# One more transpose by DMA: chunk 1's second row in a fused gated linear attention and bilinear feed-forward kernel

## The chip, the cores and the metric

The kernel runs on one core of one Trainium2 chip. The time is device microseconds (us) of one execution; three executions of the kernel before took 191.68, 191.82 and 191.87 us, median 191.82. The core has engines that each run their own instructions in order: TensorE (PE in the profile, its weight loads PEld), VectorE (DVE), ScalarE (ACT), GpSimd (POOL) and SyncE (SP, which here only issues transfers). Engines wait for one another through semaphores. Transfers are carried by 16 DMA engines, which the queues of SP, POOL and ACT share.

## The reference

The first part is a recurrence over 768 tokens for each of 4 batch rows and 8 heads, with a 48x48 state for each head; the second is a bilinear feed-forward over all 3072 tokens.

```python
def _attn_ref(q, k, v, alpha):              # each (4, 8, 768, 48), float32
    state = np.zeros((B, H, D, D), dtype=np.float32)
    for t in range(S):
        state = alpha[:, :, t, :, None] * state + np.einsum('bhd,bhe->bhde', k[:, :, t], v[:, :, t])
        y[:, :, t] = np.einsum('bhd,bhde->bhe', q[:, :, t], state)
    return y

def _moe_ref(x, w_a, w_b, w_out):           # x: (3072, 384); w_a, w_b: (384, 1536); w_out: (1536, 384)
    a = x @ w_a
    b = x @ w_b
    return a * b @ w_out
```

## The kernel before, in words

The recurrence is done in chunks. A chunk is 256 tokens (128 partitions of two tokens each) of two batch rows, called row 0 and row 1 of the chunk (`u` in the code); there are six chunks, numbered 0 to 5. Even chunks hold batch rows 0 and 1, odd ones rows 2 and 3, and chunks 2 and 3 follow 0 and 1 in time. For each chunk the kernel takes logarithms of alpha, sums them along the tokens on TensorE, raises them to decay factors, multiplies queries and keys with these, turns queries and keys so that the head dimension lies on partitions, forms masked scores, and adds the part inside the chunk and the part carried by the state. The result is evicted as the bf16 tile `xT`, and the feed-forward of that chunk follows: 12 blocks of 128 hidden columns, each with an `a` product, a `b` product, an elementwise product of both, and at last four output products with `w_out`.

The order of the work is written out. `PROGRAM` is a text in which every line names a chunk and lists its steps; the loop at L1033 emits them one by one, and each engine executes its own in that order. A step's letters V, S, P, Y say which engine runs it (VectorE, ScalarE, GpSimd, SyncE); a number at the end names the PSUM bank where a TensorE step writes. A step that writes a bank waits until the readers of what was there are done. The steps that matter here, with the functions that emit them:

- `ld a 0 P`, `ld k * Y`: load alpha, k, q or v of row 0, row 1 or both (`*`); L515. Row 0a and 0b in chunk 0 are halves of the heads. Loads of `W` (w_a, w_b; L495) and `Wo` (w_out; L498) are issued by POOL.
- `ln` (L522, ACT): logarithms. `l2`, `l2s` (L530, L579): sums over token pairs. `H`, `L`, `R`: their split into high and low parts. `B`, `A2`, `AQ`: running sums on TensorE. `E .. b` and `E .. i` (L633, ACT): decay factors and inverse factors. `ra` (L611, ACT) and `lv` (L618): the level of a token's first half. `dk`, `de`: decay of a whole sub-chunk.
- `mk`, `mq` (L644, DVE): multiply keys and queries into `QKp`.
- `C u h` (L704) turns half the heads of one row with eight TensorE transposes into a PSUM bank; `Ce u h` (L928 on DVE, L926 on ACT) evicts that bank into `kqT`. `T u` (L713) turns a whole row instead by one DMA transpose issued by SP from `QKp` into `kqT`, and `Tr u` reorders its keys into the tile `kp` (L928 or L926). In the kernel before, chunks 0 and 1 use `C` and `Ce`, chunks 2 to 5 use `T` and `Tr`.
- `v`, `vs` (L737 or L739, L926 or L928): values as bf16 and their swapped copy. `K`, `K2` (L760, L773): state products, `k` (L787, L790, L791): state update on DVE.
- `D u h` (L805): scores. `M` (L814): masked eviction on DVE; or `Mc` (L818, ACT) and `Mm` (L822, DVE) in two steps. `SB`, `SA`, `Y` (L834): the parts of the attention output. `X` (L870 on ACT, L872 on DVE): eviction to `xT`.
- `a f w`, `b f w` (L889): feed-forward products of block f, of one row of tokens (`a 3 0`: 128x256, a half product) or both (`a 3 *`: 128x512). `as` (L895, ACT) evicts `a`; `pr` (L903, DVE) multiplies it with `b` out of PSUM. `o m h` (L911): output product of token block m, first or second six blocks. `ot` (L926, L928) evicts it, `st` (L944, SP) stores it. `oc`, `otc`, `stc` do the same for the last block in two column halves.
- `fill`: products of zeros in the first microseconds.

Which of the two queues a load stands in decides what it follows. POOL executes its arithmetic steps (`lv`, `l2`) and its load issues in one order, so a load behind an `lv` on POOL is issued only when that `lv` has its operands. SP's queue holds transposes, stores and the later loads, and an issue behind a `T` waits until that `T` was issued.

## Time and profile before

| | before |
|---|---|
| median of three executions | 191.82 us (191.68 to 191.87) |
| the profiled execution | 191.33 us, of which its span is 189.5 us |
| TensorE busy | 183.1 us (97% of the span) |
| VectorE busy | 135.3 us (71%) |
| ScalarE busy | 117.2 us (62%) |
| GpSimd busy | 57.7 us (30%) |
| moved by DMA | 29.41 MB |

The profile shows one execution. Busy time of TensorE includes the modelled end of each product in a pipeline, so a busy TensorE is not one at its peak; how fast it really goes is read from when one group of products starts after the other in the timeline. The profiled execution took 0.49 us less than the median of the three others.

### The profile page before, as it was taken

The page shows a single profiled execution, that of the slowest core. Times are in us where ns is not written, and L with a number is a line of the kernel's source. Part 1 is how long each engine was busy: PE and PEld are TensorE (multiplying, and loading weights), DVE is VectorE, ACT ScalarE, POOL GpSimd, SP SyncE. Part 2 cuts the span into 40 slices and gives each one's busy share as a digit, 9 for nine tenths or more (in the row PEclk, how much of TensorE's full clock was granted, in tenths as well). Part 3 has the DMA queues.
Part 4 walks back from the last instruction along what each step waited for, and adds up shares of the span by engine and source line. Part 5 has one row for each costly group of instructions (what it writes and reads, how often), then busy time and mean ns, then how long its engine had stood idle before and what let it go on. Part 6 is the DMA issues. An engine that isn't in the chain of part 4 may idle for free.

```text
span 189.5 us, 6112 instructions
## 1 busy us (share of the span) xinstructions
PE 183.1 (97%) x2597; PEld 114.6 (60%) x2613; DVE 135.3 (71%) x246; ACT 117.2 (62%) x220; POOL 57.7 (30%) x81
## 2 busy tenths in 40 slices
PE   7999899999999999999999999999999999999993
PEld 3888676656688776644457544646446454545563
DVE  2477778679898999797899898995287753144511
ACT  4497586896978996667475979747625524320610
POOL 8999177985154000203930226002000000000000
PEclk9999999999999999999999999999999999999999
DMA  5999999999999799988999396926902100002123
GB/s 130 265 223 199 263 241 248 237 258 268 236 220 194 102 190 263 266 231 154 208 267 206 93 159 134 127 85 71 175 27 83 45 3 0 0 5 83 42 83 125
DMA packets 64475, 29.41 MB, mean 155 GB/s; under 512 B 55760, under 2 KB 62816, under 8 KB 64448
## 3 DMA queue, kind: packets, MB, share of 16 engines
q1 hardware_dynamic: 46080, 16.34, 40.9%
q0 software_dynamic: 18224, 12.58, 38.8%
q8 instruction: 20, 0.33, 0.7%
q10 hardware_dynamic: 144, 0.10, 0.2%
q14 instruction: 7, 0.06, 0.1%
HBM read 25.98 MB, written 4.74 MB: 162 GB/s over the span
## 4 chain that ended last, share of the span: by engine, by line
PE 88%; DMA 4%; DVE 3%; issue 2%; POOL 2%; ACT 1%; POOLq 0%; ACTq 0%
PE psum L889 47%; PE psum L911 24%; PE psum L834 6%; DMA a_t<-in_alpha_dram 4%; PE psum L805 2%; PE psum L704 2%; PE psum L599 1%; DVE prod L903 1%; PE psum L922 1%; PE psum L773 1%; PE psum L760 1%; PE psum L666 1%; PE psum L557 1%; PE psum L558 1%; DVE vx L928 1%
## 5 line engine op out<-in xcount | busy, mean ns | idle before, releaser
L889 PE MATMUL psum<-xT,wb_t 128*128 128x512 bf16 (+1 forms) x261 | 54.7, 335 | 1.1 <-DVE vx L928 0.4
L889 PE MATMUL psum<-xT,wa_t 128*128 128x512 bf16 (+1 forms) x264 | 54.7, 336 | 0.4 <-issue 0.2
L911 PE MATMUL psum<-wo_t,prod 128*128 128x384 bf16 x276 | 49.2, 326 | 0.1
L889 PEld LDWEIGHTS <-wa_t 128*128 128x128 bf16 x270 | 25.8, 98 | 20.1 <-issue 0.2
L889 PEld LDWEIGHTS <-wb_t 128*128 128x128 bf16 x270 | 25.6, 98 | 19.6 <-DMA wb_t<-in_moe_w_b_dram 0.7
L911 PEld LDWEIGHTS <-prod 128*128 128x128 bf16 x276 | 26.2, 98 | 17.9
L926 ACT ACTIVATE ot<-psum 128x384 f32<-128x384 f32 (+1 forms) x12 | 5.7, 478 | 17.9 <-PE psum L911 15.3
L618 POOL TENSOR_TENSOR q_t<-q_t,ra 128x384 f32<-128x384 f32 x7 | 7.0, 1007 | 28.0 <-ACT ra L611 26.9
L926 ACT ACTIVATE vx<-v_t 32x384 bf16<-32x384 bf16 x28 | 14.6, 521 | 0.5
L579 POOL TENSOR_TENSOR l<-la 64x384 f32<-64x384 f32 x6 | 6.0, 994 | 26.0 <-PE psum L889 11.3
L818 ACT ACTIVATE m<-psum 128x768 bf16<-128x768 f32 x14 | 11.0, 810 | 3.2 <-PE psum L805 3.1
L928 DVE COPY ot<-psum 128x384 f32<-128x384 f32 (+1 forms) x13 | 7.0, 536 | 7.5 <-PE psum L911 7.0
L814 DVE TENSOR_TENSOR m<-psum,mask 128x768 bf16<-128x768 f32 x10 | 9.5, 952 | 1.8 <-PE psum L805 1.2
L522 ACT ACTIVATE la<-a_t 128x1536 f32<-128x1536 f32 (+2 forms) x9 | 9.4, 1053 | 2.0 <-DMA a_t<-in_alpha_dram 2.0
L870 ACT ACTIVATE xT<-psum 128x768 bf16<-128x768 f32 x10 | 7.9, 811 | 4.1 <-PE psum L834 3.9
L644 DVE TENSOR_TENSOR QKp<-q_t,beta 128x768 bf16<-128x768 f32 x10 | 9.4, 952 | 0.6 <-POOL q_t L618 0.6
L644 DVE TENSOR_TENSOR QKp<-k_t,invb 128x768 bf16<-128x768 f32 x10 | 9.6, 968 | 0.4 <-ACT invb L633 0.2
L834 PE MATMUL psum<-m,vx 64*64 64x64 bf16 (+1 forms) x576 | 8.7, 205 | 0.0
L515 POOL DMA_DIRECT2D v_t<-in_v_dram x8 | 8.7, 1087 | 0.0
L834 PEld LDWEIGHTS <-vx 64*64 64x64 bf16 x576 | 7.6, 108 | 0.6 <-issue 0.5
L737 ACT ACTIVATE vx<-v_t 128x768 bf16<-128x768 bf16 x9 | 7.5, 838 | 0.3 <-DMA v_t<-in_v_dram 0.2
L822 DVE TENSOR_TENSOR m<-m,mask 128x768 bf16<-128x768 bf16 x14 | 7.4, 551 | 0.4 <-ACT m L818 0.3
(278 smaller groups left out, 300.5 us busy)
## 6 DMA issues: line engine op xcount, KB each, us to landing
out_dram<-ot SPq DMA_DIRECT2D x23, 192.0 KB, 2.0
q_t<-in_q_dram SPq DMA_DIRECT2D x3, 768.0 KB, 6.0
k_t<-in_k_dram SPq DMA_DIRECT2D x3, 768.0 KB, 12.1
a_t<-in_alpha_dram POOLq DMA_DIRECT2D x2, 768.0 KB, 11.9
v_t<-in_v_dram POOLq DMA_DIRECT2D x4, 384.0 KB, 8.2
a_t<-in_alpha_dram SPq DMA_DIRECT2D x2, 768.0 KB, 6.7
a_t<-in_alpha_dram POOLq DMA_DIRECT2D x3, 384.0 KB, 7.8
k_t<-in_k_dram POOLq DMA_DIRECT2D x3, 384.0 KB, 7.4
```

The costliest lines, as they stand in the source:

```text
L515: eng.dma_start(out=t[:, us, hs].rearrange("p b h r d -> p (b h) (r d)"), in_=src[ch.b0 + us.start:ch.b0 + us.stop, hs, ch.s * 2 * C:(ch.s ...
L522: nc.scalar.activation(out=ch.la[:, us, hs].rearrange("p b h r d -> p (b h r d)"), in_=ch.a[:, us, hs].rearrange("p b h r d -> p (b h r d) ...
L644: eng.tensor_mul(QKp[ch.c % 2][:, u, j, :, hs, :D], src[:, u, hs].rearrange("p h r d -> p r h d"), f)
L737: nc.scalar.activation(out=o_, in_=i_, func=AF.Copy)
L814: nc.vector.tensor_mul(m, x, maskn())
L818: nc.scalar.activation(out=m, in_=x, func=AF.Copy)
L834: nc.tensor.matmul(o, lhsT=lhsT, rhs=rhs, start=(g, c) not in begun, stop=False, skip_group_check=True)
L870: nc.scalar.activation(out=o_, in_=i_, func=AF.Copy)
L889: nc.tensor.matmul(p, lhsT=(wa_t, wb_t)[w][:, kk, f * 128:(f + 1) * 128], rhs=ch.xT[:, kk, us, :], start=(kk == 0), stop=(kk == KT - 1))
L911: nc.tensor.matmul(op, lhsT=ch.prod[:, f, at:at + C], rhs=wo_t[:, f, :], start=(f == 0), stop=(f == NFF - 1))
L926: nc.scalar.activation(out=o_, in_=i_, func=AF.Copy)
L928: eng.tensor_copy(o_, i_)
```

## The change

The functions are the same; only `PROGRAM` differs. For chunk 1's row 1 the steps `C 1 1`, `C 1 0`, `Ce 1 1 V` and `Ce 1 0 V` are gone, and `T 1` (a DMA transpose on SP) and `Tr 1 V` (on DVE) take their place. Chunk 2's keys (`ld k *`) are no longer loaded from POOL's queue but from SP's, behind that transpose. The loads of chunk 3's alpha and values, and of its queries and keys, stand later in the order. Besides, every step has been placed anew: order, PSUM banks and, for some 60 steps, the engine. Counted over the whole text, VectorE takes over from GpSimd a net six `lv` and four `l2` or `l2s`, ScalarE takes over from VectorE `vs` and `ot` steps, and the `X` steps are distributed anew. The feed-forward products, their shapes and their number are the same.

The diff, cut to the first 25 us or so of the kernel, to chunk 1's attention, and to the loads that move:

```diff
-0: ld q 0b Y; B 0a 0; E 0b i; mk 0b V; ld v 0 P; ld q 0a Y; ld a 1 P; cs 0 m P; ld k 1 P; ld q 1 P; cm 1; E 0b b; dk 0 2; E 0a i; mq 0b V; C 0 1 3; W b 0 256; cz 0 v P
-0: ld v 1 P; mk 0a V; E 0a b; fill 2 0; W a 256 768; cz 1 q P; W a 0 256; mq 0a V; C 0 0 1; Ce 0 1 S; Ce 0 0 V; K 0 0 0; de 0; W b 256 768; D 0 1 2; D 0 0 4; cs 1 m P; ln 1
-0: k 0 0 V; SB 0 0
-1: ld a 0 P
-0: v 0 S; vs 0 1 S; B 1a 6; E 1a i; M 0 0
-1: ld a 1 P
-0: E 1a b; W a 768 1536; c2 P; vs 0 0 V; B 1b 4; W b 768 1536; dk 1 6; E 1b i; M 0 1
-1: ld q 0 P
-0: Y 0
-1: ld k 0 P
-0: mk 1a V; SA 0; E 1b b; mq 1a V; mk 1b V; C 1 0 7; K 1 1 2; mq 1b V; Ce 1 0 V; C 1 1 3; v 1 S; Ce 1 1 V; de 1; K 1 0 4; k 1 0 V; k 1 1 V; D 1 0 6; X 0 S
-0: a 2 0 0; a 4 0 1; Mc 1 0; vs 1 1 V; as 4 0; vs 1 0 V; a 5 0 3; D 1 1 4; Mc 1 1; SB 1 6; Mm 1 1 V; a 1 0 1; Mm 1 0 V; b 4 0 2; as 1 0; pr 4 0; a 3 0 4; as 3 0
-0: b 0 0 1; K 0 1 5; SA 1; Y 1; a 0 0 2; as 2 0; b 2 0 0; k 0 1 V; X 1 S; b 3 0 4; pr 3 0
-1: ln 0; l2 0 P
...
+0: B 0a 0; ld q 0b Y; E 0b i; E 0b b; mk 0b V; ld v 0 P; ld q 0a Y; ld a 1 P; cs 0 m P; mq 0b V; ld k 1 P; ld q 1 P; fill 2 2; cm 1; W b 0 256; E 0a i; dk 0 3; mk 0a V
+0: E 0a b; cz 0 v P; C 0 1 2; Ce 0 1 S; mq 0a V; C 0 0 0; Ce 0 0 V; ld v 1 P; de 0; W a 256 768; cz 1 q P; K 0 0 1; ln 1; D 0 1 4; D 0 0 2; k 0 0 V; SB 0 0; M 0 0
+0: v 0 S; vs 0 1 S; dk 1 6; de 1; M 0 1; W a 0 256; B 1a 2; vs 0 0 S; E 1a b; mq 1a V; W b 256 768; E 1a i; mk 1a V; B 1b 4; E 1b i; mk 1b V; Y 0; E 1b b
+0: SA 0; X 0 V; C 1 0 2; v 1 S; vs 1 1 S; K 1 0 3; K 1 1 4; cs 1 m P; a 5 0 5; as 5 0; Ce 1 0 V; D 1 0 0; Mc 1 0
+1: ld a 0 P
+0: a 3 0 2; as 3 0; mq 1b V; C 1 1 5; vs 1 0 S; k 1 0 V
+1: ld a 1 P
+0: a 0 0 3; W a 768 1536; a 4 0 0; as 4 0; k 1 1 V; a 1 0 2; Ce 1 1 V; SB 1 4; Mm 1 0 V; D 1 1 6; Mc 1 1; Mm 1 1 V
+1: ln 0
+0: b 3 0 0; pr 3 0; b 5 0 1; pr 5 0; a 2 0 6; c2 P; as 0 0; SA 1; W b 768 1536
+1: ld q 0 P; l2 0 P
+0: Y 1; X 1 V; b 2 0 7; b 1 0 0
+1: ld k 0 P
+0: b 0 0 1; pr 0 0
...
-2: ld k * P
...
-3: ld v * P
...
-3: ld a * P
-1: mk 1 V; D 0 1 4; M 0 1
...
-1: C 1 1 2; C 1 0 4
-0: ot 3 V
-1: Ce 1 1 V
...
-1: K2 1 1 5 7; Ce 1 0 V; D 1 1 2; Y 0; v 1 S; SA 0
...
+1: Y 0; mk 1 V; mq 1 V; T 1; SA 0; K2 1 1 2 3; X 0 S; v 1 V; vs 1 0 S; vs 1 1 S
+0: o 3 1 -
+1: a 7 0 4; a 9 0 5; a 10 0 6; as 10 0; k 1 0 V; k 1 1 V
+2: l2s 0 V
+0: c3 P
+1: a 2 0 2; b 9 0 3
+2: ld k * Y; ld v * P
+0: o 2 0 7
+1: b 2 0 6
+0: ot 3 S; st 3 Y
+1: b 10 0 0
+2: l2s 1 V; l2 0 V; R 0
+1: as 2 0; pr 2 0; as 7 0; pr 10 0
+0: ot 1 S
+2: ra 0; lv 0 q P
+1: b 7 0 2
+2: ra 1
+1: pr 7 0; a 6 0 4; as 6 0; b 6 0 6; pr 6 0; as 9 0
+3: ld a * P
+0: o 2 1 -; ot 2 S
+1: a 0 0 2; Tr 1 V
+3: ld v * P
+1: as 0 0
+0: cs 1 0 P
+1: pr 9 0; b 0 0 0
+2: R 1
+1: D 1 1 4; SB 1 6; pr 0 0
+0: st 0 Y
+1: Mc 1 1; Mm 1 1 V; a 1 0 1; as 1 0; a 4 0 2; as 4 0; a 3 0 3; as 3 0; D 1 0 4; M 1 0
+2: AQ 0; E 0 b; E 0 i; lv 1 k V
+1: b 1 0 2; b 4 0 3; pr 4 0
...
```

## The prediction

> **What bounds the kernel now.** I read the page's busy shares first, then the chain that ended last, then who waited, and last the timeline of the first 25 us.

> ```profile
> PE 183.1 (97%) x2597; PEld 114.6 (60%) x2613; DVE 135.3 (71%) x246; ACT 117.2 (62%) x220; POOL 57.7 (30%) x81
> PE 88%; DMA 4%; DVE 3%; issue 2%; POOL 2%; ACT 1%; POOLq 0%; ACTq 0%
> ...
> PE psum L540 <- DVE og L440: 1.2, 1, 1.2
> PE psum L889 <- issue: 0.5, 3, 0.2
> PE psum L889 <- DVE vx L928: 0.4, 1, 0.4
> ```

> TensorE is the bound: it is 88% of the chain, and all its waits come to 2.3 us. From about 22 us to its end at 186.5 us, group follows group in the timeline: a half product starts 0.33 us after the last, a full one 0.65, an output group of six 0.98. So a change can gain only by taking products from TensorE or by getting through the first 22 us sooner, and it loses wherever TensorE begins to wait. The other engines have little in hand:

> ```profile
> core 0: us, PE busy (x) PEld busy (x) DVE busy (x) ACT busy (x) POOL busy (x), PEclk, DMA share, GB/s
> ...
> 40.00:50.00 10.00, 10.00 (x186) 6.62 (x185) 9.50 (x17) 8.09 (x13) 5.70 (x7) 1.00 1.23 257
> 50.00:60.00 10.00, 10.00 (x160) 8.01 (x159) 9.05 (x19) 8.83 (x21) 3.66 (x4) 1.00 1.39 219
> 60.00:70.00 10.00, 10.00 (x158) 8.08 (x156) 9.41 (x25) 9.15 (x20) 1.43 (x2) 1.00 0.97 140
> ```

> VectorE is 91 to 95% busy here, and from 40 to 60 us the DMA share is above 1: more transfers are outstanding than 16 engines carry. The granted clock is 1.00 throughout, so no step below turns on it.

> **The change, part by part.** *1. The sixteen transposes.* Chunk 1's `C 1 1` and `C 1 0` leave TensorE:

> ```profile
> 45.09 1.06 PE L704 MATMUL psum<-ident,QKp 128*128 128x128 bf16 x16
> 45.98 1.14 PE L911 MATMUL psum<-wo_t,prod 128*128 128x384 bf16 x6
> 45.86 1.28 DVE L928 COPY kqT<-psum 128x1024 bf16<-128x1024 bf16 x2
> ```

> In the chain they are 0.89 us, by the neighbours' starts 0.85 to 1.0. They lie on the path: −0.9. DVE loses 1.3 us of evictions and gains `Tr 1` (kp row, 0.51), and is not the bound.

> *2. The first 25 us.* I lay the new order end to end, each step from its operands on and at the spacing at which the same step follows another here.

> ```profile
> 9.16 1.02 ACT L926 ACTIVATE kqT<-psum 128x1024 bf16<-128x1024 bf16 x1 [0.52 <-PE psum L704]
> 12.34 0.61 DVE L928 COPY vx<-v_t 32x384 bf16<-32x384 bf16 x2
> 13.41 0.87 ACT L633 ACTIVATE prod<-psum 128x384 f32<-128x384 f32 x2
> 16.76 0.81 ACT L870 ACTIVATE xT<-psum 128x768 bf16<-128x768 f32 x1
> 18.09 1.16 PE L889 MATMUL psum<-xT,wa_t 128*128 128x256 bf16 x9
> 20.57 0.50 PE L889 MATMUL psum<-xT,wb_t 128*128 128x256 bf16 x3 [0.43 <-DVE vx L928]
> ```

> The rows are the first `Ce`, `vs 0 0`, the first factors of row 1, `X 0`, the first feed-forward products, and the first `b`, which waited for w_b. In the new order both fills (0.27 each) and `dk 0` stand ahead of `C 0 1`, so `Ce 0 1` starts at 9.7, not 9.16. ACT then does `de 0`, `ln 1` (10.95), `v 0`, `vs 0 1`, `de 1`, and at 13.9 `vs 0 0`, which DVE did before and which costs ACT 1.05. So row 1's first factors start at 15.0, not 13.4. DVE multiplies at 15.4, 15.9 and 16.4 and does `X 0` from 16.9 to 17.8; `a 5 0` starts at 17.85, near the 18.09 of before. But `D 1 0` and `C 1 1`, which stood ahead of it, now come after it. `D 1 0` waits 0.3 for `Ce 1 0`; `Y 1` waits 0.45 for `D 1 1`, `Mc 1 1` (0.81) and `Mm 1 1` (0.47). At 24.8 us the new order has finished 12 half products with `K 0 1` to come, the old one 12.4 with `K 0 1` done. That is 0.13 + 0.37 = 0.5, and a bank that `pr 5 1` frees 0.1 late: +0.55. Ends: −0.1 if the 0.7 us that TensorE lost before about the first `b` is won in full, +1.2 with whole durations in place of spacings.

> *3. More joints.* TensorE changes from long products to groups of 64x64 products 30 times in place of 27; one such group costs 0.06 to 0.25 more than its products (`SB` alone 0.14). Part of this is in step 2: +0.2 (0 to 0.6).

> *4. The new wait.* `T 1` starts when `mq 1` ends. Laid out on from step 2, TensorE reaches `Y 0` at 46.05 us and DVE does `M 0 1`, `mk 1` and `mq 1` (0.88 each) from 44.75 to 47.4. On SP's queue nothing is ahead of it; behind it stand chunk 2's keys, two stores, the decay rows of chunk 2 and its own transposes. On DVE, `pr 9 0`, `R 1` and `pr 0 0` stand behind `Tr 1`, and TensorE's `D 1 1` needs `Tr 1`. TensorE has `Y 0`, `SA 0` and `K2` (1.2 together), three output groups and twelve half products before it: 1.2 + 2.9 + 3.9 = 8.0, so it arrives at about 54.1, and `T 1` has to land by 53.6. The rows of a transpose and of a crowded DMA:

> ```profile
> 129.10:136.90 7.80, 7.64 (x83) 4.00 (x71) 2.94 (x4) 5.62 (x10) 0.99 (x2) 1.00 0.95 137
> 48.00:52.00 4.00, 4.00 (x74) 2.49 (x63) 3.52 (x7) 3.90 (x8) 0.25 (x1) 1.00 1.50 233
> DMA to landing us min/median/max: 4.4/4.7/4.8
> ```

> The landing row is the transposes' own; two of them, nearly alone, held the 16 engines 0.95 of 7.8 us, some 3.6 us each. At 47.4 chunk 2's queries (issued at 37.2, landing 11.1 us later) and then its values are still in flight; the values take some 2.7 us. Sharing engines, both are through at 48.3 + 2.7 + 3.6 = 54.6. `Tr 1` then ends at 55.1, and `D 1 1` is 1.0 late: +1.0. Ends: 0 if it lands in 4.8 us; +2 if the values and a store go first as well. This cover is the only one that the change adds and the only one that I think fails. [...]

> *5. Everything else.* Chunk 2's keys follow `T 1` on SP; loads behind a transpose landed 3 us apart there, so at about 57.7, and `lv 1 k` on DVE is due at about 58: 0, with the failure as a rival. The later loads of chunk 3 are hidden by some 5 us of other work each; if that cover went, ACT's `ln` would be late and with it `AQ`. Moved steps add to DVE six `lv` (0.555), four `l2`/`l2s` (0.57), two `v` (0.35), one `X` (0.96), one `Tr` and take four `vs` (0.53), five `ot` (0.55) and two `Ce` (0.69): +1.5 us in all. ACT gets some 6 us more and POOL 13 less, both below their share; the end (last eviction and store, 186.5 to 189.5) is as before. Costed at 0 (0 to +1).

> Sum: −0.9 + 0.55 + 0.2 + 1.0 = +0.85 us. The profiled execution's 191.33 becomes 192.18; the median stands 0.49 above it, so 192.67, forecast **192.7 us**.

> **Rivals.** *The transpose is hidden* (faster or equal). `T 1` lands in the 4.4 to 4.8 us of its row; it decides at 6.2 us after issue. For it: one of the eight transposes went out at 57.9 us, beside a load, and its queue was free again 3.07 us later. Against it: the share of 1.50. Without step 4 the sum is −0.15; with step 2 at its low end −0.8; the middle, −0.45, gives 191.4. [...]

> *The keys are late too* (slower still). If `T 1` lands at 54.6 and chunk 3's alpha, which POOL issues once `ra 0` is done, shares the engines from 55.5 on, the keys land at about 60, not 57.7. DVE stops at `lv 1 k`, `pr 1 0` behind it does not free its bank, and TensorE stops at `a 11 0`: +1 to +2, 193.7 to 194.7. Against it: half of the alpha's issue may come late enough.

> *VectorE becomes the bound.* 91% from 40 to 130 us and +1.5 us with less idle to place it in: a few short waits that are not won back, +1 to +2 without step 4's wait; 193. Against it: the evictions that leave are in that very stretch.

> That the change does not do what it says is excluded: sixteen transposes are gone from TensorE's list and one DMA transpose more is on SP's.

> **How the numbers follow.** Forecast (+0.4 to +1.4): 0.36. Hidden: 0.42, of which 0.28 faster by over 0.2% (0.38 us, about what a measurement of this kernel can tell from no change) and 0.14 within. Keys late: 0.16. VectorE: 0.06. The low ends of the forecast and of VectorE's case lie within 0.2% with 0.04 more. So faster 0.28, same 0.18, slower 0.54. Range 191.2 to 194.4: below it a tenth (the hidden case with step 2 at its low end), above it a tenth (late keys at their upper end). The forecast's own range is 192.2 to 193.2.

> **What would show it.** Step 1: 48 rows of L704 transposes in place of 64, and nine transposes on SP. Step 2: `X 0` on DVE near 17 us, and a gap in TensorE's starts before `Y 1`. Step 4: `kp` on DVE waiting for the transpose by name, a landing above 6 us, and TensorE's scores of chunk 1's row 1 behind it. The prediction is wrong if TensorE's starts have no gap between 45 and 60 us, or if it is behind by more than 1 us at 25 us.

## The result, and the profile after

The changed kernel took 197.4 us at the median of four executions (196.25 to 200.21), the kernel before 191.84 beside it: a ratio of 1.0257 (95% interval 1.0209 to 1.0305). The ratio leaves out the execution of 200.21 us, which is over 1.5% above the fastest. By it the change is slower by 4.9 us, where 0.85 was forecast, and outside the range of 191.2 to 194.4 us. In its first profiled execution the granted TensorE clock stood at one half for 6.8 us, and that execution is the 200.21; so the same kernel was profiled once more, and what follows is from that second profile unless it says otherwise.

> The changed kernel once more, with nothing edited. Its first profile had the granted clock at one half from about 13 to 20 us, while its other runs (196.3 to 198.0 us) had a clock of 1.0; so a profile at full clock is wanted. Theory W (three waits that the new order makes): 196.5 to 197.5 us again, and at full clock TensorE loses about 1.3 us more than before up to the first feed-forward product, 1.5 at `a 9 *` near 33 us, 1.5 at `1 o 3 1` near 78 us, 0.6 at `3 Y 1` and 1.2 at chunk 4's `D 1 0` near 130 us. Rival C (the clock): the half-clock stretch comes back in the profile, and it is the loss: 2.8 us or more of the 5 lie at `B 1a` and `B 1b`.

Measured: 196.5 us (195.7 to 198.4), ratio 1.0227 (1.0164 to 1.0290); the profiled execution is the 198.4. First its page: the span, the busy shares, the clock by fortieths of the span, the chain that ended last, and the group of the output products.

```profile
span 196.6 us, 6102 instructions
...
PE 186.8 (95%) x2597; PEld 115.1 (59%) x2597; DVE 135.1 (69%) x245; ACT 123.8 (63%) x234; POOL 44.7 (23%) x66
...
PEclk9988999999999999999999999999999999999999
...
PE 86%; DMA 3%; ACT 3%; issue 2%; DVE 2%; SPq 1%; DVEq 0%; ACTq 0%
...
L904 PE MATMUL psum<-wo_t,prod 128*128 128x384 bf16 x276 | 50.0, 326 | 2.0 <-issue 2.0
```

The half clock is not the whole of the loss: two of these executions had a mean clock of 1.0 and took 195.7 and 196.2 us. So rival C above, that the clock is the loss, falls as the only cause.

VectorE, ScalarE and GpSimd are all less than 70% busy: none of them has become the bound. In the chain TensorE's share fell from 88% to 86%, and "issue", time in which TensorE waited for nothing that the profile shows, ends 2.0 us ahead of output products. The busy time by stretch of the same run:

```profile
core 0: us, PE busy (x) PEld busy (x) DVE busy (x) ACT busy (x) POOL busy (x), PEclk, DMA share, GB/s
10.00:14.00 4.00, 3.54 (x95) 3.05 (x93) 2.87 (x4) 3.90 (x9) 4.00 (x8) 0.88 1.31 219
14.00:18.00 4.00, 4.00 (x66) 3.77 (x66) 1.14 (x3) 2.62 (x7) 3.95 (x6) 0.69 1.38 200
...
40.00:50.00 10.00, 9.46 (x222) 5.94 (x220) 9.12 (x20) 7.02 (x12) 1.15 (x1) 1.00 1.29 220
50.00:60.00 10.00, 10.00 (x135) 7.33 (x135) 8.58 (x18) 8.63 (x22) 3.96 (x4) 1.00 1.16 216
60.00:70.00 10.00, 10.00 (x152) 8.22 (x145) 9.04 (x20) 9.08 (x20) 1.96 (x3) 1.00 1.11 144
74.00:82.00 8.00, 6.57 (x162) 4.39 (x164) 6.84 (x14) 5.48 (x10) 0.00 (x0) 1.00 1.25 274
```

From 50 to 60 us, where the forecast put its 1.0 us of waiting, TensorE is busy throughout. It idles from 74 to 82 us instead, where the kernel before was busy 7.95 of the 8.00 us. The chain there, in the changed kernel:

```profile
78.12 0.69 PE psum L827 x60
78.81 0.76 PE psum L904 x4
79.57 1.43 issue
80.99 0.50 PE psum L904 x2
```

TensorE stops in the middle of one output group: four of its six products are issued, then nothing for 1.43 us, then the last two. The profile finds no semaphore that these two waited for.

To find all such places, each group of products was measured from its start to the next group's start, less the usual spacing of its kind (0.328 us a half product, 0.648 a full one, 0.975 an output group, and so on); what is left over is lost time. By stage, from the two profiles:

| stage (us, roughly) | lost before | lost after | what it is |
|---|---|---|---|
| to 17 | 4.15 | 6.24 | `B 1a`, `B 1b` at half clock, 0.98 + 0.90; the rest in the first steps |
| 17 to 39 | 1.22 | 1.90 | many small waits |
| 39 to 76 | 0.74 | 1.61 | 0.61 at 44.0, 0.58 at 49.3: issue |
| 76 to 83 | 0.33 | 2.03 | 1.75 at 79.2: issue |
| 83 to 125 | 0.88 | 1.55 | 0.92 at 107.5: issue |
| 125 to 146 | 0.23 | 2.07 | 1.16 at chunk 4's `D 1 0`; the rest in small waits |
| later | 0.40 | 0.18 | |
| sum | 7.95 | 15.58 | +7.6 |

The products themselves are 1.0 us less. So the end of TensorE's work comes 6.6 us later in this execution, some 1.7 of it by the clock (`B 1a` and `B 1b` took 2.28 and 2.20 us, in before 1.25 and 1.55), 3.9 by issue, 1.2 by chunk 4's `D 1 0`.

### The profile page after: what moved, and what is told of

It is laid out like the page before. It is cut to its first block, busy times and chain, and to the rows that moved or that the text cites. A ratio compares the mean times of both kernels' runs of the same rounds, so it can differ in the third digit from the quotient of the medians.

```text
span 198.4 us, 6102 instructions
## 1 busy us (share of the span) xinstructions
PE 188.1 (95%) x2597; PEld 116.4 (59%) x2597; DVE 136.2 (69%) x245; ACT 123.8 (62%) x234; POOL 44.0 (22%) x66
## 4 chain that ended last, share of the span: by engine, by line
PE 79%; DMA 7%; DVE 5%; ACT 2%; issue 2%; POOL 1%; SPq 1%; POOLq 0%; DVEq 0%; ACTq 0%
PE psum L882 42%; PE psum L904 23%; PE psum L827 5%; DMA a_t<-in_alpha_dram 4%; DMA bl<-row 3%; PE psum L798 2%; DVE prod L896 2%; PE psum L550 1%; PE psum L551 1%; PE psum L659 1%; PE psum L915 1%; PE psum L766 1%; PE psum L592 1%; DVE l L523 1%; SPq L937 1%
## 5 line engine op out<-in xcount | busy, mean ns | idle before, releaser
L882 PE MATMUL psum<-xT,wa_t 128*128 128x512 bf16 (+1 forms) x270 | 55.8, 337 | 1.3 <-DVE prod L896 1.3
L882 PE MATMUL psum<-xT,wb_t 128*128 128x512 bf16 (+1 forms) x270 | 56.3, 337 | 0.6 <-ACT as__467 L888 0.3
L919 ACT ACTIVATE vx<-v_t 32x384 bf16<-32x384 bf16 x40 | 20.8, 520 | 0.7
L919 ACT ACTIVATE ot<-psum 128x384 f32<-128x384 f32 (+1 forms) x17 | 8.2, 483 | 11.7 <-PE psum L904 8.5
L611 POOL TENSOR_TENSOR q_t<-q_t,ra 128x384 f32<-128x384 f32 x3 | 3.0, 1014 | 36.3 <-ACT ra L604 36.3
L863 ACT ACTIVATE xT<-psum 128x768 bf16<-128x768 f32 x9 | 7.1, 813 | 6.2 <-PE psum L827 6.1
L921 DVE COPY ot<-psum 128x384 f32<-128x384 f32 (+1 forms) x8 | 4.2, 528 | 8.6 <-PE psum L904 8.6
L827 PE MATMUL psum<-m,vx 64*64 64x128 bf16 (+1 forms) x576 | 8.9, 208 | 0.5 <-issue 0.5
L572 POOL TENSOR_TENSOR l<-la 64x384 f32<-64x384 f32 x3 | 3.0, 995 | 28.2 <-ACT la L515 28.2
L827 PE MATMUL psum<-kqT,Sm 64*64 64x128 bf16 x144 | 7.8, 219 | 0.0
## 6 DMA issues: line engine op xcount, KB each, us to landing
out_dram<-ot SPq DMA_DIRECT2D x23, 192.0 KB, 4.0
```

Of the source, the lines that this page charges most:

```text
L827: nc.tensor.matmul(o, lhsT=lhsT, rhs=rhs, start=(g, c) not in begun, stop=False, skip_group_check=True)
L863: nc.scalar.activation(out=o_, in_=i_, func=AF.Copy)
L882: nc.tensor.matmul(p, lhsT=(wa_t, wb_t)[w][:, kk, f * 128:(f + 1) * 128], rhs=ch.xT[:, kk, us, :], start=(kk == 0), stop=(kk == KT - 1))
L919: nc.scalar.activation(out=o_, in_=i_, func=AF.Copy)
L921: eng.tensor_copy(o_, i_)
```

## The experiments

**Which part of the new order loses.** Three kernels join the two orders: each takes its first steps from one and the others, in their own sequence, from the other.

```diff
# e2: first 177 steps of before (32 us), then the rest in the order of after
# e3: first 127 steps of after (25 us), then the rest in the order of before
# e4: first 204 steps of after (38 us), then the rest in the order of before
```

> The order of before for its first 177 steps (to about 32 us of the span), the new order for everything behind them. Theory W: the lead-in's 1.3 us and the 1.5 at `a 9 *` are gone, the waits near 78, 109 and 130 us stay: 197.4 - 2.8 = 194.6 us. Rival E (everything is lost early, the later waits only show slack that an early loss made): about 192 us. Rival L (all of it is lost late): 197 us.

> The new order for its first 127 steps (to about 25 us of the span), the order of before for everything behind them; the DMA transpose is not in it. Theory W: 191.8 + 1.3 = 193.1 us. Rival C: 195 us or more, with the clock at one half between 13 and 20 us in some runs. Rival L: 191.8 us.

> The new order for its first 204 steps (to about 38 us of the span), the order of before for everything behind them; the DMA transpose is not in it. Theory W: 191.8 + 1.3 + 1.5 at `a 9 *` = 194.6 us. Rival E: 197 us. Rival L: 191.8 us.

Measured: e2 198.1 us, ratio 1.0239 (1.0172 to 1.0307); e3 193.8, ratio 1.0071 (1.0037 to 1.0105); e4 195.9, ratio 1.0171 (1.0112 to 1.0230). The new first 25 us alone cost 1.4 us by the ratio: 0.7 to 0.9 in the five executions whose mean clock was 1.0 (their mean is 192.9 us, against a mean of 192.2 and a median of 192.0 for before), and about 2.2 in the five where it was 0.991 (194.0 to 194.5). So theory W has the order's own part about right, and theory C has a part too. Rival L, by which e3 and e4 would have stayed at 191.8 us, falls with both. e2 keeps all of the loss though its first 32 us are those of before: theory E falls. Not all of e2 tells of the change, though. At its seam TensorE lost 1.9 us (`b 8 *`, `a 6 *`); its wait near 78 us was 2.20 us, and behind it the clock stood at one half for 3.4 us. e4 loses 1.2 us at a seam of its own kind and had the half clock in three of four executions; its sum can't be divided further.

**Code loading.** In the wait at 79 us (1.43 us) the profile shows nothing that was missing, which leaves the instruction itself. The page's DMA part has a queue of that name:

```profile
q8 instruction: 20, 0.33, 0.7%
```

Twenty packets of 16,384 bytes, which the trace places all along TensorE's run; its 2597 products and 2597 weight loads are 20.3 times 256. TensorE's instructions were numbered in order (matmuls, weight loads, and the few that only wait or drain), and the four issue waits of the changed kernel fall at numbers 1216, 1472, 2496 and 3264; in its first profile at 2496 (1.5 us) and 3264 (0.65); in e2 at 2496 (2.20). All of these numbers are 192 more than a multiple of 256. A packet's transfer ends 1.73, 1.29, 1.32 and 1.55 us before TensorE goes on. The theory F that follows: code comes in blocks of 256 instructions; where a block's instructions run out sooner than the next block's transfer ends, TensorE stands still. When a block is asked for no trace had shown; that it is when the one before is entered, as the forecast for e5 has it, was the author's assumption. In the changed kernel's first profile small products (64x64, in `D`, `K2`, `SB`, `Y`: some 9 to 17 ns for each matmul with its weight load) made the block ahead of number 2496 pass in 4.1 us (77.4 to 81.5); a block of feed-forward products alone took 25.7 (158.2 to 183.9). The sharpest test shifts the blocks and leaves all work where it is:

```diff
 def ff(ch, w, f, us, i):
-    for kk in range(KT):
-        nc.tensor.matmul(p, lhsT=..., rhs=ch.xT[:, kk, us, :], ...)
+    for part_ in two halves of the columns if ch.c == 0 and n == 4 * C:   # e5: in before, 12 groups
+        for kk in range(KT):                                             # e8: in after, f in (6, 7, 8), 6 groups
+            nc.tensor.matmul(p[:, part], lhsT=..., rhs=ch.xT[:, kk, part_, :], ...)
```

> The order of before, not one step moved; the twelve full products of chunk 0 (three matmuls of 512 columns each) are issued as six matmuls of 256 columns each. The same work, 72 more instructions on TensorE before 44 us. Theory F (code loading): TensorE's instructions come in blocks of 256, the next block is asked for when one is entered, and with the DMA engines full it is usable about 5.8 us later; a block whose 256 instructions run through sooner leaves TensorE without instructions ('issue' in the waits). Shifting the block boundaries of before by 72 puts blocks 10 and 13 onto its small products: by its own start times 3.3 + 3.5 us of waits near 81 and 106 us, 0.3 near 50: 191.9 + 7 = 199 us (195 to 201, as part of it can be won back by loads that come earlier). Rivals W and C (the wait belongs to the new order, its transfers or its clock, not to the code): 191.9 to 192.3 us, since nothing that they speak of changes.

> The changed kernel, not one step moved; six of chunk 0's full products are issued as six matmuls of 256 columns instead of three of 512: 36 more instructions on TensorE before 36 us, the same work. Theory F, by the changed kernel's own start times: the waits for code near 44, 49 and 79 us shrink from 0.3, 1.1 and 1.5 us to 0, 0 and 1.0, one of 1.1 us is new near 136 us: 196.4 - 0.8 = 195.6 us, with the wait at `1 o 3 1` moved to another operation, 36 instructions earlier. Rivals W and C: 196.4 us and the wait at `1 o 3 1` as before.

Measured: e5 194.5 us, ratio 1.0127 (1.0077 to 1.0176); e8 195.6, ratio 1.0169 (1.0130 to 1.0207). The kernel before, with no step moved, became 2.4 us slower by the ratio through 72 instructions. The split in itself does not explain that: by the spacings above, two half products take 0.656 us and a full one 0.648, so twelve split groups cost an estimated 0.1 us. Its chain near 105 us:

```profile
104.30 1.46 PE psum L834 x67
105.76 1.58 issue
107.34 0.30 PE psum L834 x5
```

Its issue waits of 0.91, 0.56, 0.40 and 1.80 us are at numbers 704, 1728, 2752 and 3520, again 192 more than a multiple of 256; before has none above 0.45. The size was missed (7 us forecast, 2.4 measured, outside 195 to 201), because the forecast counted a block's time from when TensorE enters it. The transfers show that the next block is asked for earlier: in the changed kernel, in stretches of long products, its packet runs up to 3.9 us before TensorE enters the block at whose entry it was supposed to be asked for. In e8 the waits at 44, 79 and 107 us are gone, and 0.70 us at number 1472 is left. The same stretch as above, in e8:

```profile
77.89 0.69 PE psum L827 x60
78.59 1.08 PE psum L909 x6
79.67 0.63 PE psum L592 x12
```

The output group's six products are issued without a break. In the profiles e8 ends 1.8 us sooner (span 194.8 against 196.6, the same half clock at 13 us in both). Not all that the code waits cost came back: they shrank by 3.2 us (3.9 to 0.7), and the end by 1.8. Part of the rest stands in the same profile: TensorE, now sooner at chunk 3's small products, waits 0.87 us at 101.5 us for a transpose and VectorE's copy of it, a wait that the changed kernel does not have. Rivals W and C said nothing would change in either kernel; they fall for this part.

**Why a block comes late.** Two readings were left: the DMA engines are full (share 1.25 there), or the block is run through too fast.

```diff
-4: ld a * Y          (SyncE's queue, issued at 70 us)
 0: st 1 Y
+4: ld a * Y          (issued at 74.2 us)
```

> The changed kernel with one load issued later: chunk 4's alpha (768 KB, some 2.9 us of all 16 DMA engines) goes out on SyncE's queue behind the store near 83 us, not at 70 us. Theory F1 (the code block comes late because the DMA engines are full): the ninth code block is fetched 3 to 4.5 us after it is due instead of 5.6, TensorE's wait at `1 o 3 1` shrinks from 1.75 to 0.6 us or less, 196.2 - 1.1 = 195.1 us. Theory F2 (the block is run through too fast, whatever else is transferred): the wait stays at 1.2 us or more, and the time at 196.2 us.

Measured: 195.9 us, ratio 1.0186 (1.0135 to 1.0237). The load went out at 74.2 us, sooner than the text before the run has it, but behind chunk 3's queries and a store. The profiled execution is the slowest of the six (199.2 us), so only its waits are read, not its length. The wait near 79 us shrank from 1.75 to 0.25 us, and the packet, counted from when TensorE was 64 instructions short of the block before it, started after 3.9 us in place of 5.6: F1 is right about this wait. The time hardly moved; in the profile the waits at numbers 1472 and 3264 grew to 1.13 and 1.44 us, and 0.8 us of waiting for chunk 3's transpose is new at 102 us, as in e8. That both readings hold together, a short block being late only when its transfer is late too, is argued from this one profile.

**Chunk 4's decay rows.** The waits of the changed kernel between 126 and 136 us, then its chain:

```profile
DVE Sm L784 <- DMA bl<-row: 2.0, 1, 2.0
```

```profile
121.94 0.39 SPq L706
...
122.37 1.30 SPq L937
...
123.79 0.38 SPq L648
...
124.21 6.23 DMA bl<-row
...
130.56 0.29 DVE Sm L784
```

SyncE issues a transpose (L706), a store (L937) and only then the read of the rows (L648), which lands 6.2 us later beside chunk 5's values.

```diff
-4: mk 1 V; T 1  ...  2: st 1 Y; 4: dl
+4: mk 1 V; dl; T 1  ...  2: st 1 Y
```

> The changed kernel, with one step moved: chunk 4's decay rows (`dl`, two small transfers on SyncE) are read back before its `T 1` and the output store behind it, not after them. Theory W: the rows land by 126 us instead of 130.4, VectorE does not wait 2.0 us for them, TensorE does not stop at chunk 4's `D 1 0`: 196.4 - 1.2 = 195.2 us. Rival: something else is as late (TensorE's next block of instructions, or `T 1`, which now goes out 0.8 us later): 196.4 us.

Measured: 196.3 us, ratio 1.0182 (1.0146 to 1.0218). The wait is gone. The rows' read-backs of this kernel, as far as the trace tells their landing, take:

```profile
DMA to landing us min/median/max: 2.1/2.3/2.6
```

TensorE no longer stops at chunk 4's `D 1 0`, and its loss from 125 us on to 146 falls from 2.07 to 0.69. All four executions of this kernel had the clock at 0.989 to 0.991, so its median says little against a kernel with half of them at 1.0. Between the two profiles, both with the half clock, the span is 2.1 us shorter (194.5 against 196.6). Of this 1.4 us stands in the stretch of chunk 4; the issue waits, at which the edit did not aim, are 1.1 us less as well (2.7 in place of 3.9). So theory W holds here, at 1.2 to 1.4 us.

**Both together.**

> The changed kernel with two edits: chunk 4's `dl` ahead of its `T 1`, and 36 more instructions before 36 us (six of chunk 0's full products in matmuls of 256 columns). Theory F + W: at full clock 196.0 - 1.2 - 1.5 = 193.3 us, about 1.5 more where the clock falls; TensorE's waits for code under 1 us in all. Rival (something else takes their place): 194.5 us or more at full clock.

Measured: 194.15 us, ratio 1.0101 (1.0048 to 1.0154), with 1.0 us of issue waits left (0.45 at number 448, 0.56 at 1472). Two edits that touch neither the DMA transpose nor the order of the products take back 2.4 to 3.0 of the 4.9 us (from 1.0227 or 1.0257 to 1.0101). At 193.9 to 194.5 us in five of six executions it lies between the two expectations: chunk 4's transpose now lands 6.6 us after its issue, and VectorE waits 1.5 us for it.

**The half clock.** The profile's clock record changes in steps of 3.4 us. In the five profiles of kernels with the new lead-in whose steps fall at 12.9 to 13.2 us, the clock was at one half from there on; in the six whose steps fall at 11.0 to 12.4 us (two of them with the edit of e9) it was not. The stretch of small products from 9.6 to 12.9 us fills one step in the first case only. How much of the step TensorE is busy does not decide by itself: it was busy for 2.96 of the 3.42 us ahead of the fall in e1, and for 2.95 of 3.41 in a step of e16 and 2.32 of 3.41 in one of e9, neither followed by a fall. `dk 1` (32 matmuls two columns wide) stands in it ahead of `B 1a`; in before it stands behind `B 1b`.

```diff
# e9
-0: SB 0 0; M 0 0; v 0 S; vs 0 1 S; dk 1 6; de 1; M 0 1; W a 0 256; B 1a 2
+0: SB 0 0; M 0 0; v 0 S; vs 0 1 S; M 0 1; W a 0 256; B 1a 2; dk 1 6; de 1
# e13, in the kernel of e3
-0: SB 0 0; M 0 0
+0: SB 0 0; fill 4 7; M 0 0
```

> The changed kernel with one step moved: `dk 1` and `de 1` (32 matmuls two columns wide, 0.84 us) go behind `B 1a`, not ahead of it, so that the four wide fp32 products of `B 1a` start near 12.0 us instead of 12.9, as in before (11.6). Theory C (the clock's fall in the lead-in comes from the stretch of small products that ends at the granted clock's step at 13.0 us): the clock stays at 1.0 from 13 to 16.4 us in the profile and in most runs, `B 1a` and `B 1b` take 1.3 us each again instead of 2.3 and 2.2; 196.5 - 0.8 = 195.7 us, and no run near 198. Rival (the clock falls whatever stands there): the same stretch at 0.5 in about half of the runs, 196.5 us.

> The new order's first 25 us with the order of before behind it (the run that came to 193.8 us, with the mean clock at 0.991 in half of its executions), with four dummy products of 512 columns (0.86 us of TensorE work that no step needs) behind `SB 0 0`, in the stretch of small products near 11 us. Theory C (a light stretch of 3.4 us brings the half clock): the mean clock is 0.995 or more in all executions; the dummies cost 0.4 to 0.9 us of their own, 193.3 to 193.8 us, none above 194.3. Rival: about half of the executions still show 0.991, and the time is 194.3 us or more.

Measured: e9 199.5 us, ratio 1.0317 (1.0275 to 1.0358); e13 193.1, ratio 1.0046 (1.0009 to 1.0084). e9 is a miss: four of six executions had a mean clock of 0.966 to 0.991, and even at 1.0 it took 197.7 us. `B 1a` now waited 0.85 us, which `dk 1` had filled, and `C 1 0` behind it 0.69 us more for VectorE. In e13 two of twelve executions had a lowered clock, where e3 had five of ten, and its profile, with a step at 13.3 us, stayed at 1.0. The forecast had none in e13. Two of twelve against five of ten can be chance: this leans towards the light stretch and does not show it. The half clock also came elsewhere. It came right behind a long wait at 81.7 us in e2 (2.20 us of issue), at 21.5 in e11 (2.1 us for `xT`) and at 21.9 in e12 (1.9 us for w_b); in e7 it began at 56.2 us, inside the wait of 10.5 us for a transpose, and held for 17 us. The waits of 1.75 us in e1 and 1.71 in e16 had no such fall behind them. Before showed a mean clock under 0.995 in none of its 62 executions beside these runs. What exactly decides is open.

**The transpose itself.** Done alone, in the order of before:

```diff
# e7
-1: mk 1 V; D 0 1 4 ... C 1 1 2; C 1 0 4 ... Ce 1 1 V ... Ce 1 0 V; D 1 1 2 ... D 1 0 2
+1: mk 1 V; T 1; D 0 1 4 ... Tr 1 V ... D 1 0 2 ... D 1 1 1
# e12: as e7, and
-2: ld k * P; 3: ld v * P; 3: ld a * P    (GpSimd, issued at 39.8 to 43.4 us)
+2: ld k * Y behind T 1; 2: ld v * P; 3: ld a * P; 3: ld v * P later (at 52.4, 56.3, 58.5 us)
```

> The order of before with the DMA transpose alone: chunk 1's `C 1 1`, `C 1 0` and both `Ce` are replaced by `T 1` behind `mk 1` and `Tr 1`; `D 1 0` and `D 1 1` go 1.3 and 6 us later, behind feed-forward products. Chunk 2's keys stay on GpSimd's queue; every load is issued where it was. It takes 30 instructions from TensorE's list, which by theory F leaves the block boundaries of before harmless. If the transpose lands within 6 us of about 44: -0.9, 191.0 us. If it shares its engines with chunk 2's and 3's loads and lands after 51 us: 0.5 to 1.5 us of wait at `D 1 0`, 191.5 to 192.5 us.

> The order of before with the DMA transpose of chunk 1's row 1, as in the run before it where the transpose shared its engines with four loads and landed 17 us after its issue; here chunk 2's keys go behind it on SyncE's queue, and chunk 2's values and chunk 3's alpha and values are issued on GpSimd some 5 to 10 us later, behind `ra 1`. Theory D (the transpose is slow because GpSimd's loads share its engines): with only chunk 2's queries beside it, it lands within 6 to 8 us of 44, TensorE waits 0 to 1 us at `D 1 0`, and the time is 191 to 192.5 us. Rival (the transpose is slow at this place whatever runs beside it): it lands after 55 us, 198 us or more.

Measured: e7 209.9 us, ratio 1.0776 (1.0710 to 1.0842); e12 195.0, ratio 1.0147 (1.0101 to 1.0194). Neither time was the forecast one (191.0 to 192.5 us for e7, 191 to 192.5 for e12). In e7 the transpose, issued at 44.3 us, landed at 61.1 to 62.3. From 50 to 64 us:

```profile
DVE kp L920 <- DMA kqT<-QKp: 11.1, 1, 11.1
PEld L797 <- DVE kp L920: 10.5, 1, 10.5
```

and the DMA queues from 44 to 64 us (packets, MB, share of 16 engines):

```profile
q0 software_dynamic: 3678, 2.72, 86.4%
q1 hardware_dynamic: 2366, 0.92, 47.4%
```

GpSimd's queue (q0), with four loads of 384 and 768 KB outstanding, moved 2.72 MB while SyncE's (q1), with the transpose and two stores, moved 0.92. In e12, with the loads out of the way, the same transpose, issued at 48.1 us, landed 4.5 us later: theory D holds for the landing, and the rival falls. The changed kernel has the late loads too: `T 1` went out at 49.1 us and landed at 54.8. So the later loads, which the forecast treated as a side matter, are what lets this transpose land in time. In e12's profile, its slowest execution (198.3 us), a late w_b in the lead-in cost 1.9 us and two waits for masks around the two `D` 1.1 and 0.8; what the others lost is not known. It does not beat before.

Last, the transposes were put back into the new order:

```diff
# e16, in after
-1: mq 1 V; T 1 ... Tr 1 V
+1: mq 1 V ... pr 7 0; C 1 1 1; Ce 1 1 V; a 6 0 4; C 1 0 0; Ce 1 0 V
```

> The changed kernel with its first part undone: chunk 1's row 1 is turned on TensorE again (`C 1 1`, `C 1 0` behind `b 7 0` and `a 6 0` near 54 us, with their evictions on VectorE), `T 1` and `Tr 1` are gone; all else stays in the new order, chunk 2's keys on SyncE too. Theory F: TensorE works 0.9 us more, but 32 instructions more before 56 us move the code blocks' ends: the wait near 79 us shrinks from 1.75 to about 1.2, the one at 107 us from 0.9 to 0.7, and the transfers behind `T 1` land some 3 us earlier; 196.2 + 0.9 - 0.8 = 196.3 us, between 195.5 and 196.6. Rival (the transposes are worth their full price in the new order): 197.1 us or more.

Measured: 197.7 us, ratio 1.0257 (1.0214 to 1.0301), where the change as it is had 1.0257 and 1.0227. Putting 0.9 us of work back cost between nothing and 0.6 us. The median of 197.7 us lies with the rival (197.1 or more), but the kernel before took 192.3 us beside it; by the ratio, on 191.84, it is 196.8, between the two expectations. They are not told apart. The issue waits moved as F says in kind (0.73 us in place of 1.75 at number 2496, none at 3264), but the one at 1472 grew to 1.71, and weights that landed late cost 1.9 us before 31 us in that profile.

**Combinations.** e10 puts the edits of e8, e6 and e9 together; e11 those of e8 and e6 behind the first 92 steps of before.

> The changed kernel with three edits together: 36 more instructions before 36 us (six of chunk 0's full products in matmuls of 256 columns), chunk 4's `dl` ahead of its `T 1`, and `dk 1` behind `B 1a`. Theories F, W and C each price their own part: -1.4 (code), -1.2 (rows), -0.8 (clock): 196.5 - 3.4 = 193.1 us. Rival (the waits stand in one another's shadow, so that mending one brings out the next): 194.5 us or more. If the DMA transpose and the new order were worth their 0.9 us beyond these, it would come below 191.

> The first 92 steps (19 us) in the order of before, the new order behind them, with 36 more instructions before 36 us and chunk 4's `dl` ahead of its `T 1`. By the sums of waits so far: the old lead-in has 0.7 us less than the new one up to 30 us and no half clock: 196.5 - 1.4 - 1.2 - 0.8 - 0.7 = 192.4 us, less whatever the join of the two orders costs (0 to 1). If it comes below 191.5, the new order behind 19 us is worth more than the old; if it stays above 192.5, it holds losses that none of the theories names.

Measured: e10 195.0 us, ratio 1.0161 (1.0116 to 1.0206); e11 196.6, ratio 1.0231 (1.0190 to 1.0273). Both sums were missed (193.1 and 192.4). e10 came out where its rival said, at 194.5 us or more: the waits stand in one another's shadow, so that mending one brings out the next. Its chain at chunk 3's small products:

```profile
90.91 9.52 DMA kqT<-QKp
...
100.45 0.44 DVE kp L924
...
100.93 0.54 PE psum L796 x32
```

TensorE waits 1.07 us there for a transpose and VectorE's copy of it, a wait that the changed kernel does not have. e10 is slower than e14, which has the same edits without e9's; that step's own waits in the lead-in (0.80 and 0.69 us) and this one stand in e10's profile and not in e14's, and how much each takes of the 0.8 us between the two medians is not known. e11 lost 2.1 us at its seam (TensorE waited for `xT` at 19 us, and the half clock followed); above 192.5 us it also holds, by its own text, losses that no theory names. Neither beats before, and nothing found points to a kernel that would.

## Why the prediction was wrong, point by point

*Step 1, the sixteen transposes (-0.9).* Right in what leaves TensorE. The transposes' rows of the changed kernel, on TensorE and on SyncE:

```profile
L697 PE MATMUL psum<-ident,QKp x48: 219/219/230, 9.2 to 43.1; 128*128 128x128 bf16 x48
...
L706 SPq DMA_TRANSPOSE kqT<-QKp x9: 1521/2972/4269, 49.1 to 139.3; - x9
...
DMA to landing us min/median/max: 4.3/5.6/6.5
```

48 in place of 64, and nine transfers. By the same spacings TensorE has 1.0 us less to do. Whether the new order ever got that gain, e16 could not tell.

*Step 2, the first 25 us (+0.55, ends -0.1 to +1.2).* The steps came where they were laid: the feed-forward was to start at 17.85 us, and in e4, whose lead-in is the new one at full clock, it starts at 17.92. At 24.8 us twelve half products were to be done, where before had 12.4; the traces have 11.7 in e3 and e4, and 12.3 in before. e3 measures the part by itself at +0.7 to +0.9 at full clock, inside the ends. What failed is the sentence that the granted clock is 1.00 throughout, "so no step below turns on it". It held for the order of before. The new lead-in brought the half clock in five of e3's ten executions, and half a microsecond more by the ratio (1.4 in all). The clock record of the profiles has two values, 1.0 and 0.5, and steps of 3.413 us. The step ahead of the fall was not an idle one: TensorE was busy for 2.96 of the 3.42 us from 9.62 to 13.04 us.

*Step 3, more joints (+0.2).* Not told apart from other small waits.

*Step 4, the new wait (+1.0).* It failed. `T 1` was forecast at 47.4 to 54.6 us and ran from 49.1 to 54.8; but TensorE, slower itself by then, reached `D 1 1` only at 56.6 and did not wait for it. That the landing was nearly hit is partly luck: it went out 1.7 us late and took 5.7 us where the step had 7.2. The rival that the transpose is hidden was right on this wait. That the transpose and chunk 2's values share the engines and end together, which the 54.6 us and the +1.0 rest on, no run shows: in the changed kernel's first profile the values were issued at 46.2 us and landed 6.4 us later, and `T 1` went out at 52.1, so the two were under way together for some 0.5 us. A price of sharing shows elsewhere, far above the step's upper end of 2 us: with four loads beside it `T 1` took 16.8 to 18.0 us to land in e7, and TensorE waited 10.5; with chunk 2's queries alone it took 4.5 in e12.

*Step 5, everything else (0, ends 0 to +1).* This is the step that carried the error: about 4.4 us at full clock (196.2 us, the mean of the four executions of the changed kernel under 197 at a mean clock of 1.0, less 191.9, the 1.0 of step 1 back and the 0.9 of step 2 off; with a fifth, 198.0 us at 0.999, some 4.8). It asked which engine was busy and which load was late, and priced both at nothing. The loads of chunk 2 and 3 were indeed hidden, and VectorE did not become the bound (69%). Two things were in neither list. First, TensorE's own instructions: 3.9 us of issue waits in the profile, which 36 or 72 instructions make or unmake (e8, e5). The new order sets the small products of chunk 2 close together, so that one block is through in 3.9 us, though before took 4.1, which is little more; and the sixteen transposes that left moved all later blocks' ends by 32 instructions. How much each of the two did is not shown. In the kernel before, such waits came to 0.38 us in one place (number 704); here there were four, of 0.58 to 1.75 us. Second, `dl` of chunk 4: a small transfer, moved behind a transpose and a store on SyncE, 1.2 us (1.4 by e6). The prediction asked what stands ahead on SyncE's queue for `T 1` and the keys alone.

*The sum.* +4.9 us by the ratio. Shown by taking the cause away: 2.4 to 3.0 by code and rows together (e14). The lead-in with its clock costs 1.4 when it stands alone (e3). With the 1.0 us of products saved there must be 1.5 to 2 us more that these two do not hold. The stages place them in small waits from 17 to 39 us and in chunk 4's late transpose, and e8, e10 and e15 in the wait for chunk 3's transpose that comes out when the code waits go; no run isolates them, and this part stays open.

The signs listed in advance partly held: the 48 rows and the nine transposes did; TensorE was behind by 1.8 us near 25 us in the profile of e1, which was the sign of a wrong step 2 and came through the half clock (0.2 us in e3 and e4 at full clock); `X 0` and the first products came where they were expected; the landing was under 6 us and the gap between 45 and 60 us was only 0.6 us, of another kind. By its own terms ("wrong if there is no gap") the prediction was wrong there.

## What to carry to other kernels

Where TensorE runs long stretches of small products while the DMA engines are full (share 1.25 from 74 to 82 us here), number its instructions. Here the waits put down to "issue" in the middle of a group, at numbers a multiple of 256 apart, fit code that had not arrived: the 1.75 us at 79 us were gone with 36 instructions more (e8) and 0.25 with one load later (e15). A reordering was then not neutral even where every data dependency was met in time, and an order without such waits can owe that to where its blocks happen to end: 72 more instructions for the same work made before 2.4 us slower (e5). Before a transfer joins a queue or changes places, list what each queue carries at that time: the transpose that landed in 4.5 us behind chunk 2's queries alone (e12) took 16.8 to 18.0 beside four large loads (e7).
